# Half of the second d_w product of each group moved from the fourth step to the third

## The chip, the cores and the metric

The kernel runs on one core of a Trainium2 chip. The metric is its time on the device, in microseconds (us), as the median of the fast runs. Fast runs are at a granted TensorE clock of 0.998 to 1.000. Names: PE or TensorE does the matmuls, ACT or ScalarE and DVE or VectorE do the rest of the arithmetic, POOL is GpSimd. "L553" is line 553 of the kernel. The granted clock is the share of TensorE's full clock that it was given.

## The reference, cut to what matters

```python
def _A_ref(x, w_r, w_i):                       # spectral branch
    X = rfft2(x.astype(float32)); X = X * (w_r + 1j * w_i)
    return irfft2(X, s=(S, D)).astype(bfloat16)
def _B_ref(x, w_gate, w_up, w_down):           # GEGLU feed-forward
    return (_gelu(x @ w_gate) * (x @ w_up)) @ w_down
g = sigmoid((x * gate_w).sum(-1, keepdims=True))
out = g * _A_ref(...) + (1 - g) * _B_ref(...)  # and, by vjp, the gradient of every input but B_x
```

S = 2048 tokens, D = 576, F = 4608. The change touches one thing in this: when the gradients of w_gate and w_up, products over all 2048 tokens, are computed.

## The kernel before

The first stage (some 970 of 1410 us) goes through 18 groups of 256 hidden columns, each in four steps of four token tiles. Counting is as in the code: groups 0 to 17; the steps are called first to fourth.

A step does, in TensorE's order: z (L413, L418), the product with grad_out; in the third step, the "tail" product of the group before (L567); xy (L422, L429), the two forward products; then "fillers", the weight-gradient products of the group before (d0 to d3 at L535, w0 to w3 at L553, in quarters of four matmuls). ScalarE takes z and xy out of PSUM, the memory into which matmuls write (da, xb, hu, q), and VectorE makes the activations and their derivative from these.

The FFT branch is cut into some 200 small "side units". Each is a few matmuls into a PSUM tile and a copy out of it by ScalarE. They are slotted between the fillers. Their tile can't simply get a second buffer: a build of this kernel with two stops, as no bank of PSUM is left. Cut from the kernel ("..." marks what is left out):

```python
def pftile(dt=F32):                  # the tile of every side unit: pool pz, bufs=1, shared with z
    return pz.tile([P, 2, 512 if dt is F32 else 1024], dt, tag="z", name="pf")
...
def ewt(tag, g):                     # one buffer for q, s and sg from group 1 on
    if tag in ("q", "s", "sg"):
        return unit([4, FG], name=tag) if g == 0 else ew.tile([P, 4, FG], BF16, tag=tag, name=tag, bufs=1)
...
# H_ew2: VectorE's chain after the sigmoid
V.tensor_tensor(xb[:], xb[:], s[:], op=ALU.mult)      # L483
V.tensor_tensor(dHu, da[:], xb[:], op=ALU.mult)
V.tensor_tensor(A[:], xb[:], hu[:], op=ALU.mult)
V.tensor_tensor(q[:], xb[:], q[:], op=ALU.mult)       # L486
if one:                                               # groups 0 and 1, and all third steps
    V.tensor_scalar(om[:], s[:], -1.0, 1.0, op0=ALU.mult, op1=ALU.add)
V.tensor_tensor(om[:], om[:], q[:], op=ALU.mult)      # L489: the last read of q
...
# a step's fillers and side units
state += [*H_ew1(g, tiles, da), da]
side_work(4.4)                       # about 4.4 us of FFT products on VectorE
jobs = carry + hs
for i, (w, f) in enumerate(jobs):
    if k < n and (at >= total * k / n - 0.45 or len(jobs) - i <= n - k):
        fft_next()                   # the next side unit
        k += 1
    ...
    f()                              # a part of a filler; its last part also copies the product out
    at += w
...
sigs()                               # the sigmoids on ScalarE and the chain above
```

Of the kernel before, what the change touches and what calls it, by code (L numbers as in the profile page):

```python
# [44 lines left out]
def eo(c):  # L45

    return slice(256 * (c % 2) + c // 2, 256 * (c % 2) + 256, 2)
# [208 lines left out]
def kernel(  # L256
# [246 lines left out]
    def wevac(out, in_):  # L503
        wcopy[0](out, in_)  # L504
# [3 lines left out]
    def dwtile(name):  # L508
        if not spare:
            return stage.tile([P, 2, FG], BF16, tag="dw", name=name)  # L510
        spare.append(spare.pop(0))
        return ew.tile([P, 4, FG], BF16, tag=spare[-1], name=name, bufs=2)[:, 0:2, :]

    def W_units(g):
        fsl = slice(g * FG, (g + 1) * FG)
        kt = kept[g]

        def tl(k, t):
            tile_ = kt[t // 4][min(k, 1)]
            return tile_[:, t % 4, :] if k == 0 else tile_[:, t % 4, k - 1, :]  # L520
        dwd_tiles, wp = {}, {}

        def halves(f, us):
            return [(us, lambda: f(0)), (us, lambda: f(1))]

        def wtile(key):
            if key not in wp:
                wp[key] = pw.tile([P, TPB, FG], F32, tag="wps", name="wps")
            return wp[key]

        def u_dwd(fch, h):
            def f(half):
                wps = wtile(("d", fch, h)).rearrange("p a b -> p (a b)")
                for t in range(8 * half, 8 * half + 8):
                    nc.tensor.matmul(wps[:, :288], lhsT=tl(0, t)[:, fch * P:(fch + 1) * P],  # L535
                                     rhs=dB[:, t, h * 288:(h + 1) * 288], start=(t == 0), stop=(t == T - 1))
                if half == 0:
                    return
                if h == 0:
                    dwd_tiles[fch] = stage.tile([P, D], BF16, tag="dwd", name="dwd")  # L540
                dwd = dwd_tiles[fch]
                wevac(dwd[:, h * 288:(h + 1) * 288], wps[:, :288])
                if h == 1:
                    r0 = g * FG + fch * P
                    wst[0].dma_start(out_6[r0:r0 + P, :], dwd[:])
            return halves(f, 1.0)

        def u_dw(c, cuts=(0, 4, 8, 12, T)):

            def f(t0, t1):  # L550
                wps = wtile(("w", c))
                for t in range(t0, t1):
                    nc.tensor.matmul(wps[:].rearrange("p a b -> p (a b)"), lhsT=xn[:, t, c * P:(c + 1) * P],  # L553
                                     rhs=kt[t // 4][1][:, t % 4].rearrange("p k f -> p (k f)"), start=(t == 0), stop=(t == T - 1))
                if t1 < T:
                    return
                dw = dwtile("dw")
                wevac(dw[:], wps[:])
                for k, ov in enumerate((o4v, o5v)):
                    wst[0].dma_start(ov[:, c, fsl], dw[:, k, :])  # L560
            return [(3.45 * (b - a) / T, lambda a=a, b=b: f(a, b)) for a, b in zip(cuts, cuts[1:])]

        def tail():
            wps = wtile("t")
            for t in range(T):
                for k, r in ((1, LO), (2, HI)):
                    nc.tensor.matmul(wps[r, 0, :], lhsT=xn[:, t, 512:576], rhs=tl(k, t),  # L567
                                     start=(t == 0), stop=(t == T - 1))
            dw = dwtile("dwt")
            wevac(dw[:, 0], wps[:, 0, :])  # L570
            wst[0].dma_start(out_4[512:576, fsl], dw[LO, 0, :])
            wst[0].dma_start(out_5[512:576, fsl], dw[HI, 0, :])
        w = [u_dw(c, (0, 12, T)) if g == 0 and c < 2 else u_dw(c) for c in range(4)]
        d = [u_dwd(fch, h) for fch in range(FCH) for h in range(2)]
        if g == 0:
            return [[w[0][:1], w[1][:1]], [w[2]], [d[0], d[1], d[2], d[3]], [w[3][:3]], w[3][3:], {1: [w[0][1][1], w[1][1][1]], 2: [tail]}]
        return [[d[0]], [d[1], d[2], d[3]], [w[0]], [w[1], w[2]], w[3], {2: [tail]}]


    side = []  # L580
# [311 lines left out]
    for c in range(6):  # L892
        w = gwr[0:1, eo(c)] if c < 4 else gwr[0:1, 512:D]
# [92 lines left out]
    for g in range(NG):  # L986
# [3 lines left out]
        for m in range(NPR):  # L990
# [114 lines left out]
            if done[0] == n_slots or (pr >= wgT_from and pr % 2 == 0 and len(wgT_all) < 20):  # L1105
                load_wgT()
                if done[0] == n_slots:
                    load_wgT()
        carry = pend[4] if pend else []
        pend = W_units(g)  # L1110
    flush()
    assert fft_pos[0] == len(fft) and not side
# [239 lines left out]
```

## Time and profile before

| | before |
|---|---|
| time, median of the runs before the prediction | 1409.74 us (1409.46 to 1410.56) |
| TensorE busy | 1375.1 us, 98% of the profiled span |
| VectorE, ScalarE busy | 53%, 51%, most of it in the first stage |
| third steps with three side units | 12.5 to 13.9 us long |
| fourth steps with three side units | 13.7 to 14.8 us long |

The length of a step is read from the timeline, as the distance from the start of one step's z to the start of the next one's. The profile's lines on TensorE's waits, and what they mean, stand in the prediction.

### The profile page before, as it was taken

To read this page: it belongs to the slowest core of one execution; us is meant where nothing else is said; L and a number is where in the kernel's file an instruction comes from. 1 tells how busy PE (TensorE), PEld (TensorE's weight loads), DVE (VectorE), ACT (ScalarE), POOL (GpSimd) and SP (SyncE) were. 2 spreads that over 40 slices of the span, in tenths; PEclk is the share of its full clock that TensorE was granted. 3 is DMA by queue.
4 is the path that set the end of the run, shared out by engine and by line. 5 is a ranking of instruction groups with operands and counts; after the bars stand their busy time and mean duration, and the time that the engine had idled before them with its cause. 6 is when DMAs were issued, how large, how long until landed. Compare 5 with 4: busy or idle time off the path is not lost.

```text
span 1407.4 us, 25935 instructions
## 1 busy us (share of the span) xinstructions
PE 1375.1 (98%) x10182; PEld 913.4 (65%) x10272; DVE 748.7 (53%) x1408; ACT 712.3 (51%) x1309; POOL 245.4 (17%) x486
## 2 busy tenths in 40 slices
PE   8999999999999999999999999999999999999999
PEld 6556566565565556556566566555777777777777
DVE  7875655655888777885666666561000642212101
ACT  6867767777778778767777776661000000000000
POOL 3000111123353633423101111110000100000000
PEclk9999999999999999999999999999999999999999
DMA  6423435355464655556456464849999998778874
GB/s 216 124 82 111 122 110 135 89 142 160 109 155 134 154 160 155 126 150 164 124 142 174 128 164 132 197 118 278 182 195 201 222 191 167 162 160 161 159 152 90
DMA packets 510646, 214.49 MB, mean 152 GB/s; under 512 B 312538, under 2 KB 503708, under 8 KB 510524
## 3 DMA queue, kind: packets, MB, share of 16 engines
q1 hardware_dynamic: 493402, 187.44, 56.8%
q0 software_dynamic: 14912, 24.24, 6.3%
q8 instruction: 80, 1.31, 0.4%
q10 hardware_dynamic: 2210, 1.15, 0.3%
q14 instruction: 42, 0.34, 0.1%
HBM read 41.05 MB, written 93.84 MB: 96 GB/s over the span
## 4 chain that ended last, share of the span: by engine, by line
PE 55%; ACT 1%; DMA 1%; SPq 1%; DVE 1%; issue 1%; ACTq 0%
PE acc L1202 30%; PE wps L553 7%; PE xy L429 7%; PE wps L535 4%; PE z L413 4%; PE wps L567 1%; DMA wd_all<-in_B_w_down_dram 1%; PE xy L422 1%; SPq L1127 1%; PE z L418 1%; PE pf L867 1%; PE pf L869 1%; ACT ZT L844 0%; PE pf L841 0%; ACT hu L451 0%
## 5 line engine op out<-in xcount | busy, mean ns | idle before, releaser
L1202 PEld LDWEIGHTS <-pin 128*128 128x128 bf16 x3456 | 337.9, 98 | 86.5 <-issue 1.2
L553 PE MATMUL wps<-dH,xn 128*128 128x512 bf16 x1124 | 268.1, 379 | 1.5
L429 PE MATMUL xy<-wgu,xT 128*128 128x512 bf16 x1090 | 258.0, 379 | 8.5 <-issue 7.8
L429 PEld LDWEIGHTS <-xT 128*128 128x128 bf16 x1152 | 106.5, 98 | 133.0 <-issue 24.8
L553 PEld LDWEIGHTS <-xn 128*128 128x128 bf16 x1152 | 111.4, 98 | 118.4 <-issue 0.6
L1219 ACT COPY bo<-acc 128x288 f32<-128x288 f32 x32 | 12.7, 398 | 304.4 <-PE acc L1202 304.4
L535 PE MATMUL wps<-dB,A 128*128 128x288 bf16 x1152 | 154.2, 286 | 1.0 <-DVE dB L984 0.9
L560 POOL DMA_DIRECT2D out_dram<-dw x134 | 72.8, 546 | 446.8 <-ACT dw L504 421.2
L1202 PE MATMUL acc<-wgT,pin 128*128 128x288 bf16 x1152 | 143.9, 286 | 0.5 <-ACT dw L504 0.5
L1202 PE MATMUL acc<-wuT,pin 128*128 128x288 bf16 x1152 | 143.6, 286 | 0.0
L1202 PE MATMUL acc<-wd_all,pin 128*128 128x288 bf16 x1152 | 142.6, 286 | 0.0
L413 PE MATMUL z<-wdT,dOT 128*128 128x256 bf16 x1152 | 137.5, 273 | 3.6 <-ACT Xg L710 1.0
L535 PEld LDWEIGHTS <-A 128*128 128x128 bf16 x1152 | 112.1, 98 | 34.7 <-issue 1.9
L413 PEld LDWEIGHTS <-dOT 128*128 128x128 bf16 x1152 | 112.4, 98 | 26.7 <-issue 6.4
L441 ACT ACTIVATE da<-z,omg 128x256 bf16<-128x256 f32 x288 | 112.1, 472 | 17.5 <-PE z L418 16.7
L450 ACT CAST xb<-xy 128x512 bf16<-128x512 f32 x144 | 85.1, 591 | 48.8 <-PE xy L429 48.8
L1274 DVE SCALAR_TENSOR_TENSOR f32t<-gwf,dlog,b16t 128x576 f32<-128x576 f32 x16 | 13.1, 817 | 173.4 <-DMA b16t<-dxa_scr 173.4
L448 ACT ACTIVATE q<-xy 128x512 bf16<-128x512 f32 x144 | 87.6, 611 | 17.2 <-DVE xb L489 8.6
L483 DVE TENSOR_TENSOR xb<-xb,sg 128x1024 bf16<-128x1024 bf16 x48 | 33.2, 691 | 104.2 <-ACT sg L479 104.1
L451 ACT CAST hu<-xy 128x512 bf16<-128x512 f32 x144 | 87.4, 607 | 0.0
L504 ACT CAST dw<-wps 128x512 bf16<-128x512 f32 x72 | 42.2, 588 | 68.4 <-PE wps L553 57.7
L1233 DVE SCALAR_TENSOR_TENSOR b16t<-b16t,g,f32t 128x576 bf16<-128x576 bf16 x16 | 13.1, 818 | 95.8 <-DMA b16t<-a_scr 95.6
(216 smaller groups left out, 1653.5 us busy)
## 6 DMA issues: line engine op xcount, KB each, us to landing
scr<-dH SPq DMA_DIRECT2D x144, 256.0 KB, 3.5
scr<-A SPq DMA_DIRECT2D x72, 256.0 KB, 2.7
out_dram<-dw POOLq DMA_DIRECT2D x134, 64.0 KB, 2.5
wd_all<-in_B_w_down_dram SPq DMA_DIRECT2D x3, 1728.0 KB, 12.4
out_dram<-dwd POOLq DMA_DIRECT2D x34, 144.0 KB, 3.1
scr_p<-Vt SPq DMA_DIRECT2D x32, 145.0 KB, 3.0
wgu<-in_B_w_gate_dram SPq DMA_DIRECT2D x18, 256.0 KB, 4.1
wgu<-in_B_w_up_dram SPq DMA_DIRECT2D x18, 256.0 KB, 3.4
```

Source lines behind the costliest of these rows:

```text
L413: nc.tensor.matmul(zo(t), lhsT=dOT[:, ci, t, :], rhs=wdT[:, ci, :], start=(t % 4 < 2 and ci == 0), stop=False)
L429: nc.tensor.matmul(xy[k][:, t % 2, :], lhsT=xT[:, ci, t, :], rhs=wgu[:, ci, :], start=False, stop=(ci == 3))
L441: nc.scalar.activation(da[:, t, :], z[:, t % 2, t // 2, :], ACT.Copy, scale=omg32[:, 4 * m + t:4 * m + t + 1])
L448: nc.scalar.activation(q[:, h, :], xy[:, :, 0:FG], ACT.Square)
L450: nc.scalar.copy(xb[:, h, :], xy[:, :, 0:FG])
L451: nc.scalar.copy(hu[:, h, :], xy[:, :, FG:2 * FG])
L483: V.tensor_tensor(xb[:], xb[:], s[:], op=ALU.mult)
L504: wcopy[0](out, in_)
L535: nc.tensor.matmul(wps[:, :288], lhsT=tl(0, t)[:, fch * P:(fch + 1) * P], rhs=dB[:, t, h * 288:(h + 1) * 288], start=(t == 0), stop=(t == ...
L553: nc.tensor.matmul(wps[:].rearrange("p a b -> p (a b)"), lhsT=xn[:, t, c * P:(c + 1) * P], rhs=kt[t // 4][1][:, t % 4].rearrange("p k f -> ...
L560: wst[0].dma_start(ov[:, c, fsl], dw[:, k, :])
L1202: nc.tensor.matmul(acc[:, :288], lhsT=src[:, r, :], rhs=w_of(r)[:, h * 288:(h + 1) * 288], start=(first and r == 0), stop=(last and r == F ...
```

## The change

Its intent is to even out the two steps: the third has one product as filler (w0), the fourth two (w1, w2). Half of w1 goes to the third. "Cover", below, is the time of other matmuls between a side unit and the next use of the one tile: while they run, ScalarE can empty it.

```diff
-        return [[d[0]], [d[1], d[2], d[3]], [w[0]], [w[1], w[2]], w[3], {2: [tail]}]
+        return [[d[0]], [d[1], d[2], d[3]], [w[0], w[1][:2]], [w[1][2:], w[2]], w[3], {2: [tail]}]
```

## The prediction

> **What bounds the kernel now.** I read the page's busy shares first, then the forty slices, then the waits of TensorE in the stage that the change touches, then that stage's timeline.
>
> ```profile
> PE 1375.1 (98%) x10182; PEld 913.4 (65%) x10272; DVE 748.7 (53%) x1408; ACT 712.3 (51%) x1309; POOL 245.4 (17%) x486
> DVE  7875655655888777885666666561000642212101
> ACT  6867767777778778767777776661000000000000
> PEclk9999999999999999999999999999999999999999
> ```
>
> TensorE is busy for 1375.1 of 1407.4 us, in every slice and at the granted clock. The change adds and removes no instruction, so all it can win is TensorE's idle time, and only in the first 27 or so slices (35.2 us each), where VectorE and ScalarE also work. The last 470 us are a pure stream of matmuls and are not touched.
>
> That first stage is 18 groups (0 to 17) of four steps. Each step computes one block of hidden activations, then runs weight-gradient products of the group before ("fillers"), with pieces of the FFT slotted between ("side units"). A side unit is a few matmuls into one PSUM tile, which ScalarE then empties. That tile (tag z, program names pf and z) has a single buffer, shared by all side units and by z, the first product of the next step. Over the steady part of the stage, TensorE waited for:
>
> ```profile
> PE xy L429 <- issue: 7.0, 44, 0.2
> PE pf L596 <- ACT ve L616: 1.8, 4, 1.1
> PE pf L705 <- ACT Xx L710: 1.7, 4, 0.8
> PE pf L867 <- ACT ZT L844: 1.4, 2, 1.1
> PE pf L705 <- ACT Xg L710: 1.2, 2, 0.6
> PE z L413 <- ACT Xg L710: 1.0, 2, 0.5
> ```
>
> Apart from "issue" (a constant 0.16 us a step), every line is that tile: a side unit, or z, waiting until ScalarE has emptied the unit before. The third step of group 6 shows how (times from the timeline, TensorE first, then ScalarE):
>
> ```profile
> 359.07 0.41 PE L705 MATMUL pf<-Vp,Btab 128*128 128x289 bf16 x2
> 359.31 1.89 PE L553 MATMUL wps<-dH,xn 128*128 128x512 bf16 x8
> 361.96 0.41 PE L705 MATMUL pf<-Vp,Btab 128*128 128x289 bf16 x2 [0.76 <-ACT Xx L710]
> 362.20 1.02 PE L553 MATMUL wps<-dH,xn 128*128 128x512 bf16 x4
> 363.74 1.47 PE L413 MATMUL z<-wdT,dOT 128*128 128x256 bf16 x12 [0.51 <-ACT Xg L710]
> ...
> 360.00 0.60 ACT L451 CAST hu<-xy 128x512 bf16<-128x512 f32 x1
> 360.63 1.28 ACT L710 CAST Xx<-pf 64x578 bf16<-64x578 f32 x2
> 362.40 1.29 ACT L710 CAST Xg<-pf 64x578 bf16<-64x578 f32 x2 [0.49 <-PE pf L705]
> 363.71 0.59 ACT L504 CAST dw<-wps 128x512 bf16<-128x512 f32 x1
> ```
>
> The unit of 359.07 is emptied only at 361.91, because ScalarE is still copying the activations; the next one waits, and z after it has only four filler matmuls to hide a 1.29 us copy. The printed idle under-counts a wait by about 0.17 us, because a 512-column matmul is modelled 379 ns long but the next starts 216 ns after it. So I took start-to-start distances instead, less columns/2.4 ns, over all steps from group 2 on. Waits at side units and at z come to 10.5 us in third steps, 2.0 in fourth, 2.0 in first and 1.8 in second ones. The third step is the poor one: it has one product as filler (16 matmuls, 3.45 us), the fourth has two.
>
> **What the Trainium skill says.** "Perfetto Trace Analysis", section "Matmuls", advises rotating matmul groups through different PSUM banks so that one's evacuation overlaps the next one's matmuls; the single z tile is the opposite case, and the waits above are its price. "PSUM — Partial Sum Buffer", section "Engine vs sequencer instructions", says that ScalarE's queue is strict FIFO; the trace agrees: the copy of the unit of 359.07 starts only after the cast of 360.00. "TensorE: Matmul & The Clock Gate", section "Back-to-back issue gap", gives N/2.4 + 2.5 ns for an isolated warm matmul, 216 ns at 512 columns, and about 131 ns sustained. Here 16 of them took 3.62 us with the last one's 0.38, so 3.24/15 = 216 ns: the first figure holds, and a filler matmul is worth 0.216 us of cover.
>
> **The change, part by part.** From group 2 on (group 1 still runs group 0's separate list), eight of the 16 matmuls of w1, the second product, move from the fourth step to the third. Nothing is added: 8 x 0.216 = 1.73 us leave one step and enter the one before. The order of instructions of the changed kernel confirms this and shows what else moves: the side units of both steps are spread again over six quarters of filler. With three units in the step, the cover (before the second unit, before the third, before z) goes in third steps from 1.73, 1.73, 0.86 to 2.59, 1.73, 1.73 us, in fourth steps from 3.45, 1.73, 2.59 to the same 2.59, 1.73, 1.73. With four units: third 1.73, 0.86, 0.86, 0.86 to 1.73, 1.73, 0.86, 1.73; fourth 2.59, 1.73, 1.73, 1.73 to the same. The accumulator of w1 is now open across the step's end, but its two-buffer pool is used in the same order, and w0 is copied out earlier.
>
> Third steps, group by group, from the copy times of the trace (0.65 us for most units, 1.28 for L710, 1.04 for ZT) and ScalarE's place in its queue, waits before to after: group 2 0.4 to 0, group 3 0.7 to 0.1, group 4 1.0 to 0.2, group 5 1.15 to 0.5 (its two turned tables still have 0.86 between them), group 6 1.75 to 0.15, group 7 0.6 to 0.1, group 8 0.7 to 0, group 9 1.75 to 0.15, group 13 1.45 to 0.5, group 14 0.35 to 0, group 15 0.65 to 0. Sum 10.5 to 1.7: a gain of 8.8 us. Groups 10, 11, 12, 16 and 17 have no such wait.
>
> Fourth steps: 2.0 us before, in groups 8 and 10. There ScalarE first waits for VectorE to free the one q buffer (rival two below). A longer third step frees q earlier in the fourth, but w1 is now copied out (0.6 us) ahead of the second unit's copy: I put group 8 at 1.3, group 10 at 0.8, group 7 at 0.2, and group 14 (five units) at 0.75, about 3.0. A loss of 1.0 us.
>
> **Rivals.** One: the waits move whole into the fourth step, which becomes what the third was; no gain, 1409.7. For it: in the fourth step ScalarE has two copies of w and two sigmoids (2.12 us against 1.06). Against it: the first steps already have 2.59, 1.73, 1.96 of cover, two sigmoids and two copies, and in groups 8 to 12 they do not wait at all.
>
> Two: VectorE becomes the bound. In groups 6 to 11 it has 4.5 to 5.2 us of side products in most steps, and its chain ends late in the next step:
>
> ```profile
> ACT q L448 <- DVE xb L489: 8.4, 5, 2.6
> 363.74:377.20 13.46, 13.25 (x74) 6.87 (x76) 11.82 (x24) 9.00 (x16) 2.19 (x4) 1.00 0.14 40
> 377.20:389.42 12.22, 12.17 (x78) 7.07 (x78) 11.39 (x23) 9.90 (x17) 8.26 (x17) 1.00 0.65 164
> ```
>
> (The windows are the fourth step of group 6 and the first of group 7: start and end, length, then busy PE, PEld, DVE, ACT, POOL.) VectorE is busy 11.82 us in a step of 13.46 that will last about 11.7. What it doesn't finish delays q, and so ScalarE and the tile, in the next step. Following the chain (after its first operation 2.2 us, products, then 3.4 to the release of q), only group 7's first two steps get it clearly late, by about 2 us: I charge 1.8 us. If the lag spread through groups 7 to 11, it would cost four times that, and the time would be 1409. If instead the longer third step absorbs it all, 1402.
>
> Three: the steps that do not wait now start to. The 0.86 us cover inside fourth steps of four units is new; at such places the trace has waits from 0 to 0.5 us. Six such steps at 0.3 would take 2 us; I counted about none, as ScalarE has caught up by then in the fourth step.
>
> **Range and chances.** 8.8 - 1.0 - 1.8 = 6.0 us, at TensorE's rate one to one, as nothing else ends the kernel: 1409.7 - 6.0 = 1403.7 us. The best case is the whole 8.8 with the lag absorbed, near 1401; rivals two and three together leave about 3 us, 1407. Two per cent is 28 us, and all side-unit waits of the stage together are 16.3 us, so over 2% either way is as good as excluded: what could slow it so much is a wait that I don't see, 1 in 100.
>
> **What would show it.** In the profile after, TensorE's waits for ACT at pf and z in third steps fall to about 2 us and each waiting one of these steps grows by less than 1.73 us; fourth steps shrink by about 1.7 us (to some 12 with three units), with waits near 3 us in sum. If ScalarE's wait for VectorE at q rises in first steps, rival two is at work; if fourth steps with three units keep 13.5 us, rival one. The prediction fails if the waits of third steps stay, since then the copies and not the cover set them.

## The result, and the profile after

| | before | after |
|---|---|---|
| median | 1409.48 us (1408.94 to 1410.56, 6 runs) | 1403.21 us (1403.08 to 1404.81, 6 runs) |
| ratio of fast runs | | 0.9957 (0.9944 to 0.9969) |

Ratios here are the mean time of one kernel's fast runs over that of the other's in the same rounds, so they are not quite the ratio of the medians. The kernel is 6.3 us or 0.4% faster, clear of the noise.

First two lines of the page of the profile after: the busy time of each engine, and VectorE's share in the forty slices.

```profile
PE 1373.5 (98%) x10187; PEld 913.6 (65%) x10272; DVE 748.9 (53%) x1408; ACT 710.7 (51%) x1309; POOL 245.1 (17%) x486
DVE  7876655655888878785666666561000742212101
```

The engines do the same work (VectorE 748.7 before, 748.9 after) in a span 6.2 us shorter (1407.4 and 1401.2). What went is idle time. TensorE's waits in the first stage (who waited for whom, total us, times, longest):

```profile
PE xy L429 <- issue: 6.4, 40, 0.2
PE pf L705 <- ACT Xx L710: 1.2, 2, 0.8
PE pf L705 <- ACT Xg L710: 1.1, 1, 1.1
PE pf L596 <- ACT ve L616: 1.1, 1, 1.1
PE pf L794 <- ACT Vt L797: 0.8, 2, 0.6
```

Before, side units at L705 waited 6 times and z at L413 waited 6 times in that view (all its lines counted); now L705 waits 3 times. The waits at z for Xg and Xx (1.0 and 0.5 us) are gone.

The third step of group 6 again, TensorE and then ScalarE (start, length, engine, line, operation):

```profile
357.70 0.41 PE L705 MATMUL pf<-Vp,Btab 128*128 128x289 bf16 x2
357.95 1.89 PE L553 MATMUL wps<-dH,xn 128*128 128x512 bf16 x8
359.88 0.41 PE L705 MATMUL pf<-Vp,Btab 128*128 128x289 bf16 x2
360.13 1.89 PE L553 MATMUL wps<-dH,xn 128*128 128x512 bf16 x8
361.85 1.91 PE L413 MATMUL z<-wdT,dOT 128*128 128x256 bf16 x16
...
358.55 1.28 ACT L710 CAST Xx<-pf 64x578 bf16<-64x578 f32 x2
359.88 0.59 ACT L504 CAST dw<-wps 128x512 bf16<-128x512 f32 x1
360.36 1.29 ACT L710 CAST Xg<-pf 64x578 bf16<-64x578 f32 x2
```

The copies take what they took (1.28 and 1.29 us). But the first now runs behind a longer stretch of filler and ends at 359.83, as the next unit starts at 359.88; and the last ends at 361.65, before z at 361.85. No wait is printed in brackets any more (start-to-start distances still show 0.2 us at 359.88). Where eight filler matmuls went in (1.73 us), the step grew from 13.86 to 14.06 us only.

From the two timelines, all steps from group 2 on, as the change of length, less the 1.73 us that moved:

| steps | filler moved | change of length in sum | won or lost |
|---|---|---|---|
| third, groups 2 to 17 | 16 x 1.73 = 27.65 in | +19.11 | 8.54 won |
| fourth, groups 2 to 16 | 15 x 1.73 = 25.92 out | -24.94 | 0.98 lost |
| first | none | +1.30 | 1.30 lost |
| second | none | +0.74 | 0.74 lost |
| fourth of group 17 to the end | 1.73 out | -2.37 | 0.64 won |

The sum is 6.2 us. The first steps' loss is 0.94 in group 7 and 0.37 in group 11; the second ones' is 0.60 in group 7 and 0.13 in group 8. ScalarE's wait for VectorE at q, in the first stage after (two lines), and two windows, the fourth step of group 6 and the first of group 7 (start and end, length, busy PE, PEld, DVE, ACT, POOL; then granted clock, DMA share, GB/s):

```profile
ACT q L448 <- DVE s L489: 4.1, 4, 1.8
ACT q L448 <- DVE xb L489: 2.8, 5, 0.9
361.85:373.59 11.74, 11.58 (x68) 6.09 (x68) 10.18 (x21) 8.05 (x15) 1.08 (x3) 1.00 0.06 19
373.59:386.75 13.16, 12.38 (x79) 7.07 (x78) 12.27 (x25) 9.90 (x17) 8.46 (x17) 1.00 0.70 182
```

The line with xb is of fourth steps, where the chain ran in a third step: 8.4 us before, 2.8 now, as the longer third step leaves VectorE more time. The line with s is of first and second steps: 1.6 us before, 4.1 now. In the shortened fourth step VectorE does 10.18 us of work, where it did 11.82 before; in the next, the window of 373.59, it is busy for 12.27 of 13.16 us, where it was for 11.39. It does there what the fourth step no longer has time for.

### The profile page after: what moved, and what is told of

It reads as the page before. It is cut to its first block, busy times and chain, and to the rows that moved or that the text cites. A ratio compares the mean times of both kernels' runs of the same rounds, so it can differ in the third digit from the quotient of the medians.

```text
span 1401.2 us, 25933 instructions
## 1 busy us (share of the span) xinstructions
PE 1373.5 (98%) x10187; PEld 913.6 (65%) x10272; DVE 748.9 (53%) x1408; ACT 710.7 (51%) x1309; POOL 245.1 (17%) x486
## 3 DMA queue, kind: packets, MB, share of 16 engines
q8 instruction: 80, 1.31, 0.4%
## 4 chain that ended last, share of the span: by engine, by line
PE 56%; DVE 1%; ACT 1%; issue 0%; DMA 0%; SPq 0%; DVEq 0%; ACTq 0%
PE acc L1202 30%; PE wps L553 7%; PE xy L429 6%; PE wps L535 4%; PE z L413 3%; PE wps L567 1%; PE xy L422 1%; PE z L418 1%; PE pf L867 1%; PE pf L869 1%; ACT ZT L844 0%; PE pf L841 0%; ACT q L448 0%; DMA wdT<-wdT 0%; ACT Xg L710 0%
## 5 line engine op out<-in xcount | busy, mean ns | idle before, releaser
L413 PE MATMUL z<-wdT,dOT 128*128 128x256 bf16 x1152 | 137.5, 272 | 1.8 <-ACT ve L616 0.8
L413 PEld LDWEIGHTS <-dOT 128*128 128x128 bf16 x1152 | 112.5, 98 | 23.8 <-issue 3.0
L1274 DVE SCALAR_TENSOR_TENSOR f32t<-gwf,dlog,b16t 128x576 f32<-128x576 f32 x16 | 13.1, 817 | 172.8 <-DMA b16t<-dxa_scr 172.8
L456 DVE TENSOR_SCALAR s<-q 128x1024 bf16<-128x1024 bf16 x72 | 30.7, 426 | 67.1 <-ACT q L448 67.1
```

Source lines behind the costliest of these rows:

```text
L413: nc.tensor.matmul(zo(t), lhsT=dOT[:, ci, t, :], rhs=wdT[:, ci, :], start=(t % 4 < 2 and ci == 0), stop=False)
```

## The experiments

Twelve runs follow, eleven variants and the kernel before again, all with correct results. They ran in rounds on different chips, the kernel before beside them each time, so variants are compared by their ratio to it. The sums by step below are taken from the timelines as above. One thing to know: the very first step of the kernel lasts 14.4 us in eleven of the fourteen profiles, at a granted clock of 1.00, and 16.1 in three (p_group6, b_early_q, two_sig), at 0.89. That is 1.6 to 1.7 us of clock and not of the edit, and it is left out of these sums. Whether a run without a profile had it can't be seen but by its mean clock.

**How much to move.** One, three or all four quarters of w1 instead of two. Here one; for three it is `[:3]` and `[3:]`, for all `[w[0], w[1]], [w[2]]`.

```diff
-        return [[d[0]], [d[1], d[2], d[3]], [w[0], w[1][:2]], [w[1][2:], w[2]], w[3], {2: [tail]}]
+        return [[d[0]], [d[1], d[2], d[3]], [w[0], w[1][:1]], [w[1][1:], w[2]], w[3], {2: [tail]}]
```

> One quarter of w1 (4 matmuls) moved instead of two. My theory (TensorE waits where the cover behind a side unit is shorter than ScalarE's copy): third steps keep one stretch of 0.86 us between two side units in the groups with three units, so their waits fall from 10.5 us to about 4 only, fourth steps stay near 2 us, and the lag of VectorE in group 7 is about half (1 us). Gain 4 to 5.5 us against before, time about 1404 to 1405.5. Rival (any evening-out of the two steps does it, the place of the units doesn't matter): half of the change's 6.2 us, about 1406.4. Rival (the gain is in proportion to nothing, all from w0's copy leaving the end of the step): as the changed kernel, 1403.2.

Measured: 1406.06 us, ratio to before 0.9976. The number is the rival's (1406.4), not mine (1404 to 1405.5). The trace has the reason on my side, though: third steps keep a stretch of 0.86 us between two units, as expected, and in groups 6 and 9 the unit after it waits 1.07 us. Waits of third steps came to 6.5 us where I had put 4. So this run does not tell the theory from an even share; the next runs do. It does exclude the other rival, w0's copy (1403.2).

> Three quarters of w1 moved. My theory: third steps have no more wait to lose (1.1 us left after the change), fourth steps get covers of 1.73, 0.86, 1.73 us with three units and 0.86 throughout with four, so waits of 3 to 7 us appear there, and first steps get the fourth step's VectorE chain 0.86 us later still (1 to 3 us more). Time 1405 to 1409, slower than the changed kernel by 2 to 6 us. Rival (more filler in the third step is simply better): 1400 to 1402.

Measured: 1409.17 us, ratio 0.9996. All that was won is lost. In the timelines, third steps have nothing left to win, fourth steps wait 9.8 us in sum (3 to 7 expected), first and second ones lose 0.6 us more than with the change (1 to 3 expected). The fourth step of group 8 alone has a unit with 0.86 us of cover that waits 1.55 us.

> All of w1 moved, so the fourth step has one product and the third two: the mirror of before. My theory: the fourth step becomes the poor one and worse than the third was, because it has two sigmoids where the third has one and the third has the tail product besides; waits there 10 to 16 us, and VectorE's lag into first steps 2 to 5 us. Time 1409 to 1416, as slow as before or slower. Rival (the fourth step has slack of its own): 1401 to 1404.

Measured: 1416.45 us, ratio 1.0045, slower than before, 0.45 us above the range expected. Waits in its first stage, and ScalarE in the fourth step of group 8 (470.33 to 487.03):

```profile
PE pf L705 <- ACT da L441: 2.4, 1, 2.4
PE pf L705 <- ACT Xx L710: 2.4, 4, 0.8
...
475.07 0.59 ACT L504 CAST dw<-wps 128x512 bf16<-128x512 f32 x1 [5.84 <-DMA out_dram<-dwt]
475.55 1.06 ACT L476 ACTIVATE s<-s 128x1024 bf16<-128x1024 bf16 x1
```

The top line is new: a side unit waits for da, the copy of its own step's z. Its cause is not the theory's. ScalarE's copy of w1 (475.07) stood idle for 5.84 us, by the trace for a DMA: the copy's tile shares two buffers with that of the tail product, whose DMA GpSimd issued only at 468.60, some 9 us after the tail's copy at 459.3, and which landed 6 us later. The sigmoid and da stand behind the copy in ScalarE's queue. TensorE waits 2.43 us for them and then runs part of the step at a lower clock (0.90 over the whole step). This one step loses 5.33 us. In the other fourth steps it is mostly side units that wait, as expected. With group 8, fourth steps lost 11.9 us against before, first and second ones 6.2 (2 to 5 expected), and third ones won 10.2. The span grew by 7.7 us, so 2.4 of them come from the rest. Moving all of w1 is worse, but by how much is in part this one wait. Nor does the fourth step start with two sigmoids: as the last line shows, it starts with the third step's one (L476), and its own two run at the start of the first step. The times of 0, 1, 2, 3, 4 quarters are 1409.5, 1406.1, 1403.2, 1409.2, 1416.5 us: the change sits on the best of these five.

**Units instead of filler.** The kernel before, with one side unit of each third step that has three or more moved to the fourth.

```diff
             n = want(pr) - done[0]
+            n -= int(pr > 7 and m == 2 and n > 2)
```

> The kernel before, filler untouched, but one side unit of each third step that has three or more goes to the fourth step instead. My theory says that what counts is cover per side unit, not the length of the step: third steps lose most of their 10.5 us (to about 2), fourth steps have 2.59 and 1.73 us of cover and keep 2 to 4 us. VectorE's lag into first steps should not grow, as the fourth step keeps its length. Time about 1402 to 1404.5, as good as the change. Rival (the change worked because VectorE and ScalarE got a longer third step): the third step gets no longer here, so no gain, 1408 to 1410.

Measured: 1407.12 us, ratio 0.9983, between the two forecasts. Both halves show in the timelines. Third steps did lose their waits: in groups 6 and 9 they shrank by 1.78 us each, of which the unit taken out (0.24 us) is a small part. Cover per unit is what they lacked. But in groups 6 to 8 the fourth steps got them back: 1.08 and 0.92 us, 1.11 and 0.18, 1.99 and 0.93. ScalarE in the fourth step of group 8, which starts at 465.73:

```profile
470.75 0.59 ACT L451 CAST hu<-xy 128x512 bf16<-128x512 f32 x1
473.94 0.60 ACT L448 ACTIVATE q<-xy 128x512 bf16<-128x512 f32 x1 [2.60 <-DVE xb L489]
474.43 1.27 ACT L710 CAST Xx<-pf 64x578 bf16<-64x578 f32 x2
475.73 0.60 ACT L448 ACTIVATE q<-xy 128x512 bf16<-128x512 f32 x1
```

ScalarE stands idle for 2.60 us until VectorE's chain of the short third step has read q for the last time; the side unit's copy (474.43) is behind it in the queue. So a short third step is paid for twice: in cover, and in VectorE's time. In the first stage, these waits at q after third steps come to 12.1 us here, 8.4 before and 2.8 with the change. The change mends both, this variant only the first.

**What is left in fourth steps.** The changed kernel, with w1 copied out after the side unit that follows it:

```diff
-        def u_dw(c, cuts=(0, 4, 8, 12, T)):
+        def u_dw(c, cuts=(0, 4, 8, 12, T), late=False):
...
-                if t1 < T:
+                if t1 < T or (late and t0 < T):
...
-            return [(3.45 * (b - a) / T, lambda a=a, b=b: f(a, b)) for a, b in zip(cuts, cuts[1:])]
+            return [(3.45 * (b - a) / T, lambda a=a, b=b: f(a, b)) for a, b in zip(cuts, cuts[1:] + (T,) * late)]
...
-        w = [u_dw(c, (0, 12, T)) if g == 0 and c < 2 else u_dw(c) for c in range(4)]
+        w = [u_dw(c, (0, 12, T)) if g == 0 and c < 2 else u_dw(c, late=g > 0 and c == 1) for c in range(4)]
```

> The changed kernel, but in the fourth step ScalarE copies w1 out after the side unit that follows it instead of before. My theory of what is left in the fourth steps of groups 8 and 10 (1.4 and 0.6 us of wait): the 0.6 us copy of w1 stands in ScalarE's queue ahead of the second unit's copy. Then group 8 falls to about 0.8, group 10 to 0, other steps stay: about 1.1 us gained, 1402 us. Rival (that wait is only the late q, the copy's place doesn't matter): both stay, 1403.2.

Measured: 1403.38 us, ratio 0.9955, no gain in time. But the steps moved as expected: the fourth of group 8 from 13.34 to 12.86 us, of group 10 from 12.55 to 12.00, and nothing else in fourth steps. ScalarE in the fourth step of group 8, the changed kernel:

```profile
474.72 0.60 ACT L451 CAST hu<-xy 128x512 bf16<-128x512 f32 x1
475.19 0.62 ACT L504 CAST dw<-wps 128x512 bf16<-128x512 f32 x1
475.67 1.30 ACT L710 CAST Xg<-pf 64x578 bf16<-64x578 f32 x2
```

and the same with the late copy:

```profile
475.36 0.60 ACT L451 CAST hu<-xy 128x512 bf16<-128x512 f32 x1
475.84 1.30 ACT L710 CAST Xg<-pf 64x578 bf16<-64x578 f32 x2
477.16 0.59 ACT L504 CAST dw<-wps 128x512 bf16<-128x512 f32 x1
```

The copy of w1 did stand in the way, for half a microsecond. But the first step of group 11 gave 0.48 us back (12.79 to 13.27), because the fourth before it had become shorter still, and q later: ScalarE's wait for it rose from 0.26 to 0.74 us there. That left 0.5 us, within the spread of the runs.

**VectorE's products.** The changed kernel, with fewer side products in one step, then in all fourth steps (`side_work(3.4 if m == 3 else 5.0)`):

```diff
-                side_work(4.4)
+                side_work(2.2 if pr == 27 else 4.4)
```

> The changed kernel with the limit for VectorE's side products at 2.2 instead of 4.4 us in one step, the fourth of group 6. My theory of the 1.5 us lost in the first two steps of group 7 is that VectorE cannot finish these products in the shortened step and frees q late. Then the first step of group 7 falls back from 13.16 to 12.2 us; the products left over come later, so its second step stays at 13.4 to 14 us. Gain 0.3 to 1.2 us, time 1402 to 1403. Rival (ScalarE is late there by its own load, two copies and two sigmoids at the end of a short step): the first step of group 7 stays at 13.1, 1403.2.

Measured: 1409.40 us, ratio 0.9997: 6 us lost against the change, which I had not seen coming. The expected part happened: in the first step of group 7, ScalarE's q came at 5.50 us of the step, instead of 7.45 (5.91 in the kernel before). But the step took 17.36 us instead of 13.16:

```profile
PE pf L794 <- DVE qn L764: 3.3, 1, 3.3
387.08 3.44 PE L553 MATMUL wps<-dH,xn 128*128 128x512 bf16 x8
```

The second side unit of that step multiplies one of the postponed products. TensorE waited for VectorE to make it, 2.7 us longer than it waited there with the change. The eight matmuls behind it then took 3.44 us, not 1.89: between 387 and 391 us the granted clock was 0.57, which makes up most of the other 1.5 us. All steps together lost 4.5 us of the 6.2 by which the profile's span grew; the other 1.7 are the first step of the kernel at its lower clock. All four runs had a mean clock of 0.998, as the profiled one, so the 6 us overstate what the edit cost. So the lag of q is VectorE's, and the products cannot be put off by a step: they are wanted there.

> The changed kernel with the limit for side products at 3.4 us in all fourth steps and 5.0 in the others, because the fourth is now the short one for VectorE and the third has more room. If VectorE's lag is the cause of what first and second steps lost (2.0 us in groups 7, 8 and 11), most of it comes back: 1401 to 1402.5. If the lag only moves to another step, as VectorE has 12 us of work in steps of 12 us whatever the order: 1403 to 1405.

Measured: 1405.13 us, ratio 0.9968, 0.1 us above the second of the two forecasts. The first step of group 7 won 0.66 us and its second lost 0.75; the second of group 8 won 0.69, and the fourth of group 7 lost 1.68. VectorE's work is the same (748.8 us busy, 748.9 with the change); the lag moved to other steps and grew, by 1.6 us in sum.

**The kernel before, again.** No edit.

> The kernel before, profiled a second time. Outside the changed stage, the trace of before had one wait of 0.65 us at the first matmuls of the last part (for ScalarE's last copy) that the trace after hasn't. If it is chance (a transfer's luck), it is absent or different here; if it belongs to the kernel, it is here again. The steps themselves should repeat within 0.1 us.

Measured: one run of 1410.48 us (its state is unknown). The steps repeat: the sum of all changes from the first profile is 0.17 us. The wait in the last part is there again, and longer (1.0 us printed, 0.5 in the first profile). The kernel before with an early q (below) has it too (0.7 us). The variant with moved units, whose last part has the same instructions, has none. So it is no single chance, but it does not follow from the order of instructions alone either. The 0.64 us won after the last z are probably its absence. The traces put it down to ScalarE's last copy of a product, and that copy's own wait of 3.9 us to a DMA that loads w_down. With the units moved, the copy waits as long (3.8 us), but TensorE does not stop for it. After the change the copy has no such wait; why, no run was made to tell.

**Freeing q earlier.** A second buffer for q would be the plain test of the late q. It did not fit: the build ran out of memory, and three ways to make room (one buffer fewer for A, one unit fewer, one half-size buffer fewer) deadlocked or were still too small (the one with fewer buffers for A deadlocks). So VectorE's chain writes its product over xb instead of q, and 1 - s over hu; the operations and their order stay.

```diff
-            om = xb
+            om = hu
...
-        V.tensor_tensor(q[:], xb[:], q[:], op=ALU.mult)
+        V.tensor_tensor(xb[:], xb[:], q[:], op=ALU.mult)
...
-        V.tensor_tensor(om[:], om[:], q[:], op=ALU.mult)
+        V.tensor_tensor(om[:], om[:], xb[:], op=ALU.mult)
```

> The changed kernel with the same operations of VectorE, but the product with q is written over xb (and 1 - s over hu), so that VectorE's last read of q is its fourth operation of the chain instead of its fifth or sixth: q comes free 0.7 us earlier, 1.2 us in third steps' chains. My theory that the waits left in first, second and fourth steps of groups 7 to 11 come from the late q: first step of group 7 falls from 13.16 to about 12.4, second from 13.82 to 13.1, second of group 8 from 13.37 to 12.7, fourth of group 8 from 13.34 to 12.7, fourth of group 10 from 12.55 to 12.0, first of group 11 from 12.79 to 12.5; sum about 3.5 us, 1399.5 to 1401. Rival (ScalarE's own load sets these waits): no step moves by more than 0.2 us, 1403.2.

Measured: 1399.53 us (1399.28 to 1399.98), ratio to before 0.9929. Step by step, expected and measured:

| step | change | expected | early q |
|---|---|---|---|
| first of group 7 | 13.16 | 12.4 | 12.22 |
| second of group 7 | 13.82 | 13.1 | 13.26 |
| second of group 8 | 13.37 | 12.7 | 12.69 |
| fourth of group 8 | 13.34 | 12.7 | 12.67 |
| fourth of group 10 | 12.55 | 12.0 | 12.03 |
| first of group 11 | 12.79 | 12.5 | 12.42 |

ScalarE in the first step of group 7, the changed kernel:

```profile
381.04 0.60 ACT L448 ACTIVATE q<-xy 128x512 bf16<-128x512 f32 x1 [1.84 <-DVE s L489]
381.53 0.81 ACT L797 CAST Vt<-pf 128x580 bf16<-128x580 f32 x1
```

and with early q:

```profile
379.73 0.60 ACT L448 ACTIVATE q<-xy 128x512 bf16<-128x512 f32 x1 [0.48 <-DVE xb L486]
380.23 0.82 ACT L797 CAST Vt<-pf 128x580 bf16<-128x580 f32 x1
```

ScalarE's wait fell from 1.84 to 0.48 us, and its releaser is now L486, the operation to which the last read of q was moved. The side unit's copy came 1.30 us sooner. The first steps gave back 1.31 us, all that the change had lost in them, so this settles where that loss came from. The second steps gave back 1.25, but more than the change had lost in group 8 (0.13) and not all in group 7: there a wait of 0.57 us is left, behind a q that is still 0.42 us late.

> The kernel before with the same early release of q. My theory: waits of third steps (10.5 us) are due to short cover, not to q, as ScalarE reaches q there only at 7.36 us for another reason (the tail product ahead), so they stay within 1 us; fourth, first and second steps lose 1.5 to 2.5 us of their 3.5 us in groups 7 to 11. Time 1406.5 to 1408, and the change on top of it is then worth 6.5 to 8 us instead of 6.2. Rival (the late q is behind the third steps' waits as well): 1400 to 1404.

Measured: 1406.20 us, ratio 0.9977, 3.1 us better than before. Third steps did not move (+0.03 us in sum): their waits had nothing to do with q. Fourth and second steps won 1.89 and 1.04 us. The change on top of it is worth 6.7 us (1406.20 to 1399.53), as against 6.3 without. In the second step of group 7 it still costs 0.53 us, and in fourth steps 1.68 where it cost 0.98.

> Early release of q and w1's late copy on top of the changed kernel. If both effects are separate, fourth steps of groups 8 and 10 have no wait left, and the lag that the late copy alone handed to the first step of group 11 (0.5 us) is absorbed: 0.5 to 1 us better than early q alone, 1399 to 1400.5. If not, equal to early q alone.

Measured: 1399.19 us (1398.96 to 1400.62), ratio 0.9928. The fourth step of group 8 went from 12.67 to 12.19 us and no first step paid for it this time; that of group 10 had no wait left to lose. The medians differ by 0.3 us and the ratios hardly, so the two versions can't be told apart by their times. Either beats the changed kernel by 3.7 us or more.

**A second sigmoid for ScalarE.** The changed kernel with `one = g < 2` in place of `one = g < 2 or m == 2`.

> The changed kernel with the second sigmoid on ScalarE in third steps too (1.06 us more for ScalarE, 0.43 us less for VectorE there). If the fourth steps' late q is VectorE's doing, q comes 0.4 us earlier in them, waits of the fourth steps of groups 8 and 10 and of the first two of group 7 fall by 0.3 to 0.4 each, about 1.2 us: 1402. Rival (ScalarE is the nearer bound at the end of third steps, where it is busy 13.8 us of 14.05): z's evacuation comes later in fourth steps and they gain 0.3 to 0.7 us of wait in groups 6 and 9: 1403 to 1404.5.

Measured: 1401.97 us, ratio 0.9947: the first forecast. Fourth steps of groups 8 and 10 fell by 0.45 and 0.52 us, the first of group 7 by 0.43; its second, where 0.3 to 0.4 were expected too, did not move. Third steps did not get longer, nor did the fourth steps of groups 6 and 9, where the rival had put its loss. VectorE's 0.4 us was worth more there than ScalarE's 1.06.

## Why the prediction was right

It gave 1403.7 us; 1403.21 was measured, inside the range. Point by point:

- **Third steps: 8.8 us to be won; 8.54 were.** The groups came out near their terms too: 1.54 us in group 6 (1.6), 0.56 in group 3 (0.6), 0.79 in group 4 (0.8). They miss both ways: group 7 won 0.82 for 0.5, groups 5 and 13 won 0.18 less than their terms each. The sum is closer than they are. Shown: in groups 6 and 9 the unit variant removes these waits without lengthening the step, and early q on the kernel before leaves them. So cover behind a side unit was what third steps lacked.
- **Fourth steps: 1.0 us to be lost; 0.98 were.** In group 8 the wait rose to 1.4 us (1.3), in group 10 it fell to 0.6 (0.8), in group 14 it came to 0.75 (0.75); group 7's 0.2 did not come, and group 4 had 0.13 instead. Both causes that the prediction named there were tested apart: w1's copy in the queue (late copy: 0.5 us in each of groups 8 and 10) and the late q (early q: 0.7 and 0.5).
- **VectorE's lag: 1.8 us to be lost in group 7; 1.54 were lost there**, and 0.13 in group 8 and 0.37 in group 11, where none was expected. The lag did not spread as rival two feared at its worst. Early q shows its path: VectorE, q, ScalarE, the single tile, TensorE. It gives back all of the first steps' loss, and leaves 0.53 us of the second's.
- **Rival one** (the waits just move) is what three quarters of w1 do, and the whole, which has other losses besides. The two sigmoids that the prediction names for it run at the start of the first step, not in the fourth: that argument rested on a wrong reading. With half, fourth steps shrank by 1.72 us in groups 6, 7 and 9.
- **Rival three** (new waits behind 0.86 us of cover in fourth steps) was put at nearly nothing; one wait of 0.14 us came in group 4, and group 14's were in its own term.
- **Left out by the prediction: the end.** A wait of 0.65 us at the start of the last part is gone. The prediction took that part as untouched, and it is untouched in its instructions. The steps alone give 5.5 us for 6.0 forecast; that the sum came to 6.2 is due to this term, which nobody had forecast, and so is luck.

The first list of what to look for held as well: ScalarE's wait at q in first and second steps did rise, from 1.6 to 4.1 us.

## What to carry to other kernels

With one buffer between two engines, look at the work that the producer has between two uses of it, and not at how busy it is on average: moving 8 of the 80 or so matmuls of a step to where cover is missing won 6 us, and moving 4 more lost them again. Before moving work out of a step, ask what the other engines do in that step's time: here VectorE needed the fourth step's length. And where an engine waits for a buffer, look at which operation reads it last; writing a product over another operand cost nothing that these runs show, and won another 3.7 us.

## What the Trainium skill lacked or had wrong

- "TensorE: Matmul & The Clock Gate", section "Back-to-back issue gap": it gives about 131 ns as the sustained distance of 512-column matmuls in a stream with weight loads, and calls the 216 ns of its formula an over-count, although the same page has 215.7 ns as measured in another section. Here 16 such matmuls, each with its own weight load, started 216 ns apart at a clock of 1.00.
- "Perfetto Trace Analysis", section "Matmuls": its advice to rotate PSUM banks has no figure for what a single tile costs. Here it was 10.5 us of 1410 in third steps, and the cover needed behind a unit was more than its copy: with copies of 1.28 us, 1.73 us of filler still left waits of up to 0.92 us in third steps before, because ScalarE's queue had other work ahead.
- "Perfetto Trace Analysis" says that a matmul's drawn end is an estimate, but no page says what that does to idle times: the one printed before a 512-column matmul's successor is about 0.17 us too short, as the matmul is drawn 379 ns long and the next starts after 216. In third steps before, the printed idle times add up to 7.0 us (the constant 0.16 a step left out), and the start-to-start distances to 10.5; the 8.54 us that were won show that the second is the truer measure.
